# Four weight slots at other byte offsets, and a 2x2 product ahead of 18 runs of matrix products

## The chip, the cores and the metric

The kernel runs on one core of one Trainium2 chip. The metric is the device time of one execution in microseconds (us), the median of several runs. Engines are named as in the profile: PE (TensorE, matrix products), PEld (its weight loads), DVE (VectorE), ACT (ScalarE), POOL (GpSimd) and SP (SyncE, which issues most transfers).

## The reference

Three stages follow each other: a block-causal attention, a feed-forward with a SoLU and a layer norm, and a second feed-forward with a Mish.

```python
scores = np.where(mask, q @ k.T / 8, -1e9)       # 4 x 8 heads, 576 positions, blocks of 64
x = softmax(scores) @ v                          # -> 2304 tokens x 512
h = x @ w_in                                     # 512 -> 1024
solu = h * softmax(h)
ln = (solu - mean(solu)) / sqrt(var(solu) + 1e-6) * g_ln
x = ln @ w_out                                   # 1024 -> 512
h = x @ w2_in                                    # 512 -> 2048
out = (h * tanh(softplus(h))) @ w2_out           # 2048 -> 512
```

All inputs are float32 (some of the weights float64). The kernel keeps the precision by splitting an operand into a high and a low part and adding three products (high by high, high by low, low by high).

## The kernel before, in words

Every operation of the program is first put into a list with an engine, a cost and a priority; a planner (`Plan.order`) then simulates the engines and writes one fixed order for each. The priorities are a table of numbers. Nothing in that table or in the planner's costs is touched here.

The first feed-forward takes 128 tokens at a time. Its first product stands at L864 (output 128 x 512), the transposition of its result at L911, and its second product at L927. `moe1_x2` does the second product for 256 tokens, a group; there are nine groups g. For each group the four 128-column blocks c of the output are worked out in pairs that share a PSUM bank. A block is 8 steps kk of three products, and the planner receives it as two pieces of 12 (k0 = 0 and k0 = 4). So a bank takes 48 products and a group 96, each with a 128 x 128 stationary operand (`woh` or `wol`) and 256 columns of `lth` or `ltl` that stream. In the first two groups the planner mixes the pieces with the attention (scores L694, its products L799 and L806, transpositions L669 and L778); in the seven later groups the 96 products stand in one piece behind L864.

The second feed-forward has its weights in four slots of SBUF. Slot j holds four tiles of 7168 bytes in each partition: `w2ihj`, `w2ohj`, `w2ilj`, `w2olj` (i: first product, o: second, h and l: high and low part). `slot` lays them down, slots 0 and 1 in the pool of `open_right`, slots 2 and 3 in the pool of `open_left`. L1124 is the first product: `w2ih` or `w2il` is stationary, 384 columns of the token blocks (six in the tile `wk`, the seventh in `x7`) stream. L1248 and L1216 are the second product, in the first and in the second half of the stage: there the split activations `ch` and `cl` (or a part of `wk`) are stationary and `w2oh` or `w2ol` streams, 512 columns at L1248, 256 at L1216. In the last part of L1216 spare parts of `w2ih` and `w2il` hold the activations. L1248 comes in pieces of 18 products of one slot (24 such pieces, 6 with each slot); L1216 comes in steps of 3 or 6, and steps of several slots follow each other.

The array's tile, as the instructions give it, is 128 x 128 at L864, L911, L927, L1124, L1216 and L1248 and in all transpositions; 64 x 128 at L694; 128 x 64 at L799; 64 x 64 at L806. The products at L799 and L806 are plain float32, and each is two weight loads and two products in the trace; those of the feed-forwards are float32r and are one.

Of the kernel before, what the change touches and what calls it, by code (L numbers as in the profile page):

```python
# [10 lines left out]
F32 = mybir.dt.float32  # L11
# [67 lines left out]
class Plan:  # L79
# [11 lines left out]
    def add(self, eng, cost, fn, r=(), w=(), prio=0.0, acq=None, rel=None, lat=None, lock=False, mode=0):  # L91
        o = Op()
        o.eng, o.cost, o.fn, o.prio, o.acq, o.rel = eng, cost, fn, prio, acq, rel
        o.lat = self.LAT[eng] if lat is None else lat
        o.lock = lock or eng == POOL
        o.mode = mode
        o.seq = len(self.ops)
        d = set()
        for k in r:
            if k in self.writer:  # L100
                d.update(self.writer[k])
            self.readers.setdefault(k, []).append(o.seq)
        for k in w:
            rd = [x for x in self.readers.get(k, ()) if x != o.seq]
            d.update(rd)
            d.update(self.writer.get(k, ()))
            self.writer[k] = [o.seq]
            self.readers[k] = []
        d.discard(o.seq)
        o.deps = d  # L110

        for k, s in zip(w, acq or ()):
            self.slot[k] = s
        o.on = list({id(self.slot[k]): self.slot[k] for k in (*r, *w) if k in self.slot}.values())
        self.ops.append(o)
        return o
# [144 lines left out]
def c_dma(kb):  # L261
    return max(0.53, kb / 260.0)
# [10 lines left out]
def c_act(n, sbuf=False, acc=False, ptr=False):  # L273
    return 0.05 + n / 1170.0 + 0.04 * sbuf + 0.18 * acc + 0.09 * ptr
# [11 lines left out]
def kernel(  # L286
# [12 lines left out]
    nc = tc.nc  # L299
# [4 lines left out]
    P = 128  # L304
# [15 lines left out]
    def pri(tag, i):  # L320
        base, step = PRIO[tag]
        return base + step * i
# [22 lines left out]
    def ps(s):  # L345
        return banks[s.at // 2][:, s.at % 2, :]
# [4 lines left out]
    ident = const.tile([P, P], F32, name="ident")  # L351
# [165 lines left out]
    def split_weight(src, sk, wd, slot, dh, dl, dk, tag, idx, g=None, gk=None, need=None):  # L517
        pt = dict(prio=pri(tag, idx))
        kw = dict(rel=[slot], **pt) if slot else dict(lock=True, **pt)
        if g is None:  # L520
            add(ACT, c_act(wd, not slot), lambda: act_hi(dh(), src()), r=[sk] + ([need] if need else []),
                w=[dk + ("h",)], **pt)
            if tag == "wi":
                add(POOL, c_tt(wd), lambda: pool_lo(dl(), src(), dh()), r=[sk, dk + ("h",)], w=[dk + ("l",)], **kw)
            else:
                add(DVE, c_dve(wd), lambda: dve_lo(dl(), src(), dh()), r=[sk, dk + ("h",)], w=[dk + ("l",)], **kw)
        else:
            add(ACT, c_act(wd, not slot, ptr=True), lambda: nc.scalar.activation(
                out=dh(), in_=src(), func=AF.Copy, scale=g()), r=[sk, gk], w=[dk + ("h",)], **pt)
            add(DVE, c_dve(wd), lambda: nc.vector.scalar_tensor_tensor(  # L530
                out=dl(), in0=src(), scalar=g(), in1=dh().bitcast(F32), op0=ALU.mult, op1=ALU.subtract),
                r=[sk, gk, dk + ("h",)], w=[dk + ("l",)], **kw)

    def hl(*k):
        return [k + ("h",), k + ("l",)]
# [385 lines left out]
    def moe1_x2(g, lth, ltl):  # L921

        def mm(s, c, k0, k1):
            cs = slice(c * P, (c + 1) * P)
            for kk in range(k0, k1):
                for i, (w, x) in enumerate(((woh, lth), (woh, ltl), (wol, lth))):
                    nc.tensor.matmul(  # L927
                        out=ps(s)[:, (c % 2) * 256:(c % 2) * 256 + 256], lhsT=w[:, kk, cs], rhs=x.t[:, kk, :],
                        start=(kk == 0 and i == 0), stop=(kk == KF - 1 and i == 2))

        for c2 in range(KD // 2):
            s = Slot()
            xo = xo_r.next()
            xk = ("x2", g, c2)
            for cc in range(2):
                for k0 in range(0, KF, 4):
                    first = cc == 0 and k0 == 0
                    add(PE, 12 * 0.1175, lambda s=s, c=2 * c2 + cc, k0=k0: mm(s, c, k0, k0 + 4),
                        r=[x.key(o) for x in (lth, ltl) for o in range(2)]
                        + [y for kk in range(k0, k0 + 4) for y in hl("wo", kk)],  # L940
                        w=[xk] + ([xo.key()] if first else []), acq=[s] if first else None, prio=pri("m_2", 2 * g + 1))
            add(ACT, c_act(512), lambda s=s, xo=xo: nc.scalar.activation(
                out=xo.t, in_=ps(s).rearrange("p (a c) -> p a c", a=2), func=AF.Copy),
                r=[xk], w=[xo.key()], rel=[s], prio=pri("m_o", 2 * g + 1))
            st = add(SP, c_dma(410), lambda c2=c2, xo=xo: nc.sync.dma_start(
                out=x2_d[:, 2 * c2:2 * c2 + 2, g * 256:(g + 1) * 256], in_=xo.t),
                r=[xo.key()], w=[("x2d", g, c2)], prio=pri("store", 0))
            stores.add(st.seq)
# [25 lines left out]
    acc_d = dram.tile([P, NTILE, DM], F32, name="acc_d")  # L974
    RIGHT, MID, LEFT, HALF = "right", "mid", "left", "half"

    def slot(p, j):
        for x in "hl":
            sl_i[j, x] = p.tile([P, 2, 7, P], F32R, name=f"w2i{x}{j}")
            sl_o[j, x] = p.tile([P, 7, 2 * P], F32R, name=f"w2o{x}{j}")  # L980

    def open_right():
        at_cm.__exit__(None, None, None)
        cm = tc.tile_pool(name="m2a", bufs=1, side="right")
        p = cm.__enter__()
        opened["r"] = cm
        for j in range(2):
            slot(p, j)
        xf_r.make(p)
        x7 = p.tile([P, 2 * GT], F32R, name="x7")  # L990
        for i, r in enumerate((blk_h, blk_l)):
            r.tiles = [wk[:, GT * (2 * n + i):GT * (2 * n + i + 1)] for n in range(6)] + [x7[:, GT * i:GT * (i + 1)]]
        g_r[0].make(p, 1)
        p.tile([P, 48], F32, name="edge_f")
        cl_r.make(p, 1)
        p.tile([P, 32], F32, name="edge_g")

    def open_mid():
        ch_r.tiles = [wk[:, 12 * GT + 48:12 * GT + 48 + 7 * P].rearrange("p (a k) -> p a k", a=7)]
# [5 lines left out]
    def open_left():  # L1005
        m1_cm.__exit__(None, None, None)
        cm = tc.tile_pool(name="m2b", bufs=1, side="left")
        p = cm.__enter__()
        opened["l"] = cm
        for j in range(2, NSLOT):  # L1010
            slot(p, j)
        g_r[1].make(p, 4)
        p.tile([P, 48], F32, name="edge_h")
        ch_r.make(p)
        cl_r.make(p)
        ob_r.make(p, 1)
        ob_r.tiles += [t.rearrange("p a b -> p (a b)") for t in xo_r.tiles]
# [384 lines left out]
    for b in range(B):  # L1402
# [5 lines left out]
        while nt < NTILE and (nt + 1) * P <= (b + 1) * S:  # L1408
# [5 lines left out]
            nt += 1  # L1414
    early = len(plan.ops)
    o = add(HOST, 0.0, open_right, w=[RIGHT], prio=-1000)
    o.deps.update(heads)
    o = add(HOST, 0.0, open_mid, w=[MID], prio=-1000)
    o.deps.update(last_use)
    o.deps.add(o.seq - 1)  # L1420
    o = add(HOST, 0.0, open_left, w=[LEFT], prio=-1000)
    o.deps.update(x for x in range(early) if x not in stores)
    o.deps.add(o.seq - 1)
# [78 lines left out]
```

## Time and profile before

| | us |
|---|---|
| median of 3 runs | 777.19 (775.67 to 777.21) |
| profiled execution | 778.42 |
| its span (first to last instruction) | 776.6 |
| PE busy | 758.3 (98%) |
| DVE busy | 574.9 (74%) |
| ACT busy | 446.8 (58%) |
| POOL busy | 250.0 (32%) |

The time around the span is 1.8 us. A busy PE is not a PE at its peak: the products are pipelined, and a row's duration (280 ns for a product of 256 columns) is longer than the step from one start to the next (0.12 us). The step is the quantity to read here, either from the starts in the timeline or from a piece of the chain divided by its count.

### The profile page before, as it was taken

To read this page: it belongs to the slowest core of one execution; us is meant where nothing else is said; L and a number is where in the kernel's file an instruction comes from. 1 tells how busy PE (TensorE), PEld (TensorE's weight loads), DVE (VectorE), ACT (ScalarE), POOL (GpSimd) and SP (SyncE) were. 2 spreads that over 40 slices of the span, in tenths; PEclk is the share of its full clock that TensorE was granted. 3 is DMA by queue.
4 is the path that set the end of the run, shared out by engine and by line. 5 is a ranking of instruction groups with operands and counts; after the bars stand their busy time and mean duration, and the time that the engine had idled before them with its cause. 6 is when DMAs were issued, how large, how long until landed. Compare 5 with 4: busy or idle time off the path is not lost.

```text
span 776.6 us, 14789 instructions
## 1 busy us (share of the span) xinstructions
PE 758.3 (98%) x5496; PEld 688.9 (89%) x5496; DVE 574.9 (74%) x1217; ACT 446.8 (58%) x938; POOL 250.0 (32%) x299
## 2 busy tenths in 40 slices
PE   7898999999999999999999999999999999999997
PEld 6777778788888899999998988988988999999997
DVE  5999898999999896334425897797433679559995
ACT  5898888686666565323428554564444764354560
POOL 1587786784765233232130362222000000000000
PEclk8899999999999999999999999999999999999999
DMA  8664543335335351000376667766696682272303
GB/s 194 165 143 113 136 109 102 115 84 160 105 135 161 95 170 48 28 15 14 122 236 218 225 200 248 279 238 237 228 307 226 200 304 67 84 290 77 95 1 109
DMA packets 108839, 118.13 MB, mean 152 GB/s; under 512 B 66016, under 2 KB 77792, under 8 KB 108768
## 3 DMA queue, kind: packets, MB, share of 16 engines
q1 hardware_dynamic: 107504, 116.88, 48.0%
q8 instruction: 43, 0.70, 0.4%
q10 hardware_dynamic: 1264, 0.31, 0.2%
q14 instruction: 28, 0.23, 0.1%
HBM read 76.27 MB, written 40.89 MB: 151 GB/s over the span
## 4 chain that ended last, share of the span: by engine, by line
PE 86%; DVE 9%; ACT 2%; issue 1%; DMA 1%; SPq 0%; DVEq 0%; ACTq 0%
PE ps L1124 23%; PE ps L864 13%; PE ps L1248 13%; PE ps L927 12%; PE ps L1216 11%; PE ps L694 4%; PE ps L778 3%; PE ps L799 3%; DVE nmx L748 2%; PE ps L911 2%; ACT pt L706 2%; PE ps L806 1%; DVE kl L335 1%; PE ps L669 1%; DVE wem L454 1%
## 5 line engine op out<-in xcount | busy, mean ns | idle before, releaser
L1124 PE MATMUL ps<-wk,w2ih 128*128 128x384 f32 x576 | 147.8, 337 | 1.7 <-ACT xt L1132 1.1
L1124 PEld LDWEIGHTS ps<-wk,w2ih 128*128 128x128 f32 x576 | 102.8, 188 | 4.1 <-ACT xt L1132 1.3
L864 PE MATMUL ps<-wk 128*128 128x512 f32 x432 | 104.6, 396 | 0.0
L762 POOL TENSOR_SCALAR pt<-pt,sm 128x192 f32<-128x192 f32 (+4 forms) x160 | 90.5, 588 | 36.1 <-DVE sm L700 15.1
L511 POOL TENSOR_TENSOR wem<-wem 128x512 f32<-128x512 f32 x40 | 60.7, 1519 | 116.5 <-DVE wem L508 103.0
L706 ACT ACTIVATE pt<-ps,nmx 128x576 f32<-128x576 f32 (+4 forms) x160 | 82.4, 537 | 25.9 <-DVE nmx L748 16.0
L1124 PE MATMUL ps<-wk,w2il 128*128 128x384 f32 x288 | 96.9, 336 | 0.0
L864 PEld LDWEIGHTS ps<-wk 128*128 128x128 f32 x432 | 79.4, 188 | 17.0 <-issue 1.1
L927 PE MATMUL ps<-lth,woh 128*128 128x256 f32 x288 | 81.6, 283 | 0.0
L927 PE MATMUL ps<-lth,wol 128*128 128x256 f32 x288 | 80.9, 281 | 0.0
L927 PE MATMUL ps<-ltl,woh 128*128 128x256 f32 x288 | 80.8, 281 | 0.0
L1248 PE MATMUL ps<-w2oh,cl 128*128 128x512 f32 x144 | 56.8, 395 | 0.0
L927 PEld LDWEIGHTS ps<-lth,wol 128*128 128x128 f32 x288 | 55.0, 191 | 0.0
L927 PEld LDWEIGHTS ps<-lth,woh 128*128 128x128 f32 x288 | 54.2, 188 | 0.9 <-issue 0.5
L1216 PE MATMUL ps<-w2oh,cl 128*128 128x256 f32 x196 | 54.9, 280 | 0.0
L778 PE MATMUL ps<-ident,pt 128*128 128x128 f32 x400 | 50.2, 277 | 4.5 <-DVE kl L335 3.0
L927 PEld LDWEIGHTS ps<-ltl,woh 128*128 128x128 f32 x288 | 54.1, 188 | 0.3
L1124 PEld LDWEIGHTS ps<-wk,w2il 128*128 128x128 f32 x288 | 54.1, 188 | 0.0
L778 PEld LDWEIGHTS ps<-ident,pt 128*128 128x128 f32 x400 | 44.9, 143 | 8.0 <-DVE kl L335 2.8
L748 DVE TENSOR_REDUCE nmx<-ps 128x2 f32<-128x896 f32 (+1 forms) x64 | 41.0, 684 | 0.8
L335 DVE TENSOR_TENSOR ltl<-ps,lth 128x1024 fp32r<-128x1024 f32 x18 | 21.3, 1217 | 26.5 <-ACT lth L329 26.5
L799 PE MATMUL ps<-ptw,vraw 128*64 128x256 f32 (+1 forms) x384 | 39.8, 359 | 0.0
(172 smaller groups left out, 1934.1 us busy)
## 6 DMA issues: line engine op xcount, KB each, us to landing
blk_d<-wk SPq DMA_DIRECT2D x36, 384.0 KB, 4.0
wk<-blk_d SPq DMA_DIRECT2D x36, 384.0 KB, 5.5
wraw<-in_moe_w_in_dram SPq DMA_DIRECT2D x24, 512.0 KB, 4.4
park_d<-wem SPq DMA_DIRECT2D x20, 448.0 KB, 2.8
wraw<-in_moe_w_out_dram SPq DMA_DIRECT2D x16, 512.0 KB, 3.9
wem<-park_d SPq DMA_DIRECT2D x18, 448.0 KB, 4.5
qraw<-in_q_dram SPq DMA_DIRECT2D x30, 160.0 KB, 3.3
x_d<-xo SPq DMA_DIRECT2D x18, 256.0 KB, 2.2
```

The costliest lines, as they stand in the source:

```text
L511: add(POOL, c_tt(wd), lambda: nc.gpsimd.tensor_tensor(out=mf(), in0=mf(), in1=ex().bitcast(F32), op=ALU.mult), r=[ek], w=[mk], **pt)
L694: nc.tensor.matmul(out=dst, lhsT=a.t[hs, t * P:(t + 1) * P], rhs=m.t[hs, o + c0:o + c1], start=(i == 0), stop=(i == 2))
L706: add(ACT, c_act(EXT[t], acc=True), lambda: nc.scalar.activation(out=pp.t[:, x * EXT[t]:(x + 1) * EXT[t]] if t < 4 else pp.t[:, x * EXT[t] ...
L748: add(DVE, 2 * c_dve(512), lambda s=s, ts=ts: [nc.vector.tensor_reduce(out=nmx.t[:, :, t], in_=ps2(s)[:, :, o:o + EXT[t]], axis=AX.X, op=A ...
L762: nc.gpsimd.tensor_scalar(pp, pp, sm.t[:, x, t:t + 1], 1.0, op0=ALU.mult, op1=ALU.mult)
L778: nc.tensor.transpose(ps2(s)[:, a, o:o + P], pts[t].t[:, c * P:(c + 1) * P], ident)
L799: nc.tensor.matmul(out=ps(os_[r])[x * D:(x + 1) * D, o:o + n_], lhsT=vr.t[:, j, x, :], rhs=packs[pi].t[:, a, c0:c0 + n_], start=(i in (0, ...
L864: nc.tensor.matmul(out=ps2(hp)[:, hf, :], lhsT=x.t[:, kk, :], rhs=w[:, kk, hf * 512:(hf + 1) * 512], start=bool(first), stop=bool(last))
L927: nc.tensor.matmul(out=ps(s)[:, (c % 2) * 256:(c % 2) * 256 + 256], lhsT=w[:, kk, cs], rhs=x.t[:, kk, :], start=(kk == 0 and i == 0), stop ...
L1124: nc.tensor.matmul(out=ps(s)[:, 0:HT], lhsT=sl_i[j, w][:, c, a, :], rhs=x.t[:, mv], start=(start and c == 0 and i == 0), stop=(c == 1 and ...
L1216: nc.tensor.matmul(out=ps(acc[bi])[:, h * 256:(h + 1) * 256], lhsT=x.t[:, a], rhs=sl_o[j, w][:, b], start=(first and h == 0 and y == 0), s ...
L1248: nc.tensor.matmul(out=ps(acc[t]), lhsT=x.t[:, 2 * t + f], rhs=plain(j, w, f), start=(first and f == 0 and y == 0), stop=(last and f == 1 ...
```

## The change

Two edits. The first puts a product of two columns by two rows, of plain float32 with start and stop flags, ahead of the first piece (k0 = 0) of blocks 0 and 2 of every group: 18 products. It reads the identity matrix and writes four numbers of the bank that the run behind it overwrites. Its array tile is 128 x 32 in the built program.

The second lays an unused piece ahead of each slot, one behind slots 1 and 3, and makes one existing unused piece 32 bytes smaller.

```diff
         def mm(s, c, k0, k1):
             cs = slice(c * P, (c + 1) * P)
+            if k0 == 0 and c % 2 == 0:
+                nc.tensor.matmul(out=ps(s)[0:2, 0:2], lhsT=ident[:, 0:2], rhs=ident[:, 0:2], start=True, stop=True)
...
+    LEAD = (16, 16, 48, 16)
+    TRAIL = (96, 64)
+
     def slot(p, j):
+        if LEAD[j]:
+            p.tile([P, LEAD[j]], F32, name=f"lead{j}")
...
         for j in range(2):
             slot(p, j)
+        p.tile([P, TRAIL[0]], F32, name="edge_k")
...
-        p.tile([P, 32], F32, name="edge_g")
+        p.tile([P, 24], F32, name="edge_g")
...
         for j in range(2, NSLOT):
             slot(p, j)
+        p.tile([P, TRAIL[1]], F32, name="edge_l")
```

The pool of slots 0 and 1 is laid down from the upper end of SBUF, so it grows downwards. The byte addresses in a partition as built:

| tile | before | remainder by 64 / by 256 | after | remainder by 64 / by 256 |
|---|---|---|---|---|
| slot 0 (`w2ih0`) | 146592 | 32 / 160 | 146176 | 0 / 0 |
| slot 1 (`w2ih1`) | 175264 | 32 / 160 | 174912 | 0 / 64 |
| slot 2 (`w2ih2`) | 72384 | 0 / 192 | 72576 | 0 / 128 |
| slot 3 (`w2ih3`) | 101056 | 0 / 192 | 101312 | 0 / 192 |
| `x7` | 216224 | 32 / 160 | 216256 | 0 / 192 |
| `cl0` | 225632 | 32 / 96 | 225664 | 0 / 128 |
| `ch1` | 136064 | 0 / 128 | 136576 | 0 / 128 |
| `cl1` | 139648 | 0 / 128 | 140160 | 0 / 128 |
| `wk` (not moved) | 5824 | 0 / 192 | 5824 | 0 / 192 |

A slot's four tiles have the same remainders, since 7168 is a multiple of 256; the second product at L1248 reads `w2oh` and `w2ol` from 192 bytes behind their start.

On PE, the third group's run of L927 stands directly behind L864 before:

```order
L864 MATMUL ps_63<-wk 128x512 [waits DVE_49]
L864 MATMUL ps_63<-wk 128x512 x23
L927 MATMUL ps_64<-lth_144,woh 128x256 [waits DVE_49,Activation_49]
L927 MATMUL ps_64<-ltl_145,woh 128x256
L927 MATMUL ps_64<-lth_144,wol 128x256
L927 MATMUL ps_64<-lth_144,woh 128x256
```

and after, with the same products now at L929, on PE at the same place:

```order
L864 MATMUL ps_63<-wk 128x512 [waits DVE_49]
L864 MATMUL ps_63<-wk 128x512 x23
L926 MATMUL ps_64<-ident 2x2 [waits DVE_49,Activation_49]
L929 MATMUL ps_64<-lth_144,woh 128x256 [waits Activation_49]
L929 MATMUL ps_64<-ltl_145,woh 128x256
L929 MATMUL ps_64<-lth_144,wol 128x256
L929 MATMUL ps_64<-lth_144,woh 128x256
```

The wait for the bank is now the 2x2 product's, the wait for the split operand stays with the run. In the middle of the same group, on PE, where the second pair of blocks begins, the order before is:

```order
L927 MATMUL ps_64<-lth_144,wol 128x256
L927 MATMUL ps_64<-lth_144,woh 128x256 [waits DVE_49]
L927 MATMUL ps_64<-ltl_145,woh 128x256
L927 MATMUL ps_64<-lth_144,wol 128x256
L927 MATMUL ps_64<-lth_144,woh 128x256
```

and after, on PE at the same place:

```order
L929 MATMUL ps_64<-lth_144,wol 128x256
L926 MATMUL ps_64<-ident 2x2 [waits DVE_49]
L929 MATMUL ps_64<-lth_144,woh 128x256
L929 MATMUL ps_64<-ltl_145,woh 128x256
L929 MATMUL ps_64<-lth_144,wol 128x256
```

One run of 96 becomes two of 48, each with a 2x2 product ahead. Of the 18 new products, two stand in the first group, behind L694 and behind L806; the other sixteen stand behind products with an array tile of 128 x 128 (L864, L1124, or the run's own). On DVE, ACT, POOL and SP no instruction is added, removed or moved.

## Rows read from the trace of the kernel before

**Rows 1.** The page: engines, and the chain that ended last by engine and line

```profile
PE 758.3 (98%) x5496; PEld 688.9 (89%) x5496; DVE 574.9 (74%) x1217; ACT 446.8 (58%) x938; POOL 250.0 (32%) x299
...
PE 86%; DVE 9%; ACT 2%; issue 1%; DMA 1%; SPq 0%; DVEq 0%; ACTq 0%
```

**Rows 2.** The chain in order of time (start us, us, what), around one group

```profile
278.92 10.92 PE ps L864 x48
289.85 11.31 PE ps L927 x96
301.15 1.75 PE ps L911 x16
```

**Rows 3.** The chain between 176 and 199 us, in the first group

```profile
187.91 1.38 DVE nmx L722 x2
189.30 0.60 DVE wem L508
189.90 1.72 DVE wem L1054 x3
```

**Rows 4.** L927, 265.8 to 277.1 us: duration ns min/median/max, first and last start

```profile
L927 PEld LDWEIGHTS ps<-lth,wol x32: 192/192/192, 265.8 to 276.8; 128*128 128x128 f32 x32
L927 PE MATMUL ps<-lth,wol x32: 281/281/283, 265.9 to 276.9; 128*128 128x256 f32 x32
```

**Rows 5.** L927 likewise, 182.1 to 185.0 us

```profile
L927 PEld LDWEIGHTS ps<-lth,wol x8: 187/188/188, 182.4 to 184.8; 128*128 128x128 f32 x8
L927 PE MATMUL ps<-lth,wol x8: 276/276/301, 182.5 to 184.9; 128*128 128x256 f32 x8
```

**Rows 6.** L927 likewise, from 186.5 us, from 231.3 and from 237.8

```profile
L927 PE MATMUL ps<-lth,wol x8: 276/276/283, 186.8 to 189.2; 128*128 128x256 f32 x8
...
L927 PE MATMUL ps<-lth,wol x4: 280/281/281, 231.6 to 232.6; 128*128 128x256 f32 x4
...
L927 PE MATMUL ps<-lth,wol x4: 276/277/281, 238.1 to 239.2; 128*128 128x256 f32 x4
```

**Rows 7.** Timeline of PE (start us, us, what): from L927 to L799

```profile
178.79 0.28 PE L927 MATMUL ps<-ltl,woh 128*128 128x256 f32 x1
178.90 0.28 PE L927 MATMUL ps<-lth,wol 128*128 128x256 f32 x1
179.11 0.44 PE L799 MATMUL ps<-ptw,vraw 128*64 128x256 f32 x2
```

**Rows 8.** Timeline of PE: all of L806, then L927, first starts and last

```profile
181.42 0.80 PE L806 MATMUL ps<-ptw,vraw 64*64 64x64 f32 x20
182.15 0.39 PE L927 MATMUL ps<-lth,woh 128*128 128x256 f32 x1
182.37 0.28 PE L927 MATMUL ps<-ltl,woh 128*128 128x256 f32 x1
...
182.84 0.28 PE L927 MATMUL ps<-lth,wol 128*128 128x256 f32 x1
...
184.88 0.30 PE L927 MATMUL ps<-lth,wol 128*128 128x256 f32 x1
```

**Rows 9.** The chain: pieces of L1248 with slots 1, 2, 3 and 0

```profile
427.54 4.19 PE ps L1248 x18
...
443.28 4.17 PE ps L1248 x18
...
470.25 4.10 PE ps L1248 x18
...
480.67 4.17 PE ps L1248 x18
```

**Rows 10.** The chain: L1124 with slots 0 and 1, 2 and 3, and 0, 1, 2, 1

```profile
535.89 7.36 PE ps L1124 x42
...
559.04 8.35 PE ps L1124 x48
...
598.56 9.51 PE ps L1124 x54
```

**Rows 11.** The chain: L1216 with slots 0 and 1, then 1 and 2

```profile
639.61 2.46 PE ps L1216 x21
...
643.12 2.51 PE ps L1216 x21
```

## The prediction

> **What bounds the kernel now.** I read the page's engine line and the chain's shares first: PE is busy for 98% of the span and holds 86% of the chain, DVE 9% [rows 1]. Then the chain in order of time. From the third group on, one group is 48 products of L864, 96 of L927 and 16 transpositions, back to back, with nothing of another engine between them [rows 2]. There, time added to PE is added to the end. In the first group it is otherwise: between 176 and 199 us the chain runs through DVE [rows 3], so that what PE does more there lies beside other work. In the second feed-forward the chain is again PE alone. What counts is therefore the step from one product's start to the next.
>
> Taken that way, L927 has two paces. A run of 96 takes 11.31 us [rows 2], a step of 117.8 ns; seven groups have such a run. The run between 182 and 185 us goes from 182.84 to 184.88 in 18 steps [rows 8], 113.3 ns each. The rows tell the paces apart: in the slow one each load of `wol` takes 192 ns and a product 281 [rows 4], in the quick one 188 and 276 [rows 5]. All tiles and addresses are the same in both. The pace is thus a matter of how the run starts, and it keeps itself up.
>
> **The 2x2 products: what one costs.** The trace has no array tile of 128 x 32, but it has changes of tile. Four pieces:
> - leaving a run of 128 x 128: from the last start of L927 to L799's first, 178.90 to 179.11, 0.21 us [rows 7].
> - from the first pass of the float32 product to its second. L806 starts 181.42 and its 20 passes, in 10 pairs, end after 0.80 [rows 8]; with a last pass of 0.22 that leaves 0.58 for nine steps, 0.06 each. A stationary operand of 2 columns instead of 64 should need less; I take 0.03, between 0.01 and 0.11.
> - from the last pass to the run. L806's last pair starts at 182.00, the run at 182.15: 0.15, of which about 0.05 is the streaming of 64 columns [rows 8]. I take 0.10, at most 0.15.
> - the run's first step, in which nothing was loaded ahead: 182.15 to 182.37, 0.22 [rows 8].
>
> That is 0.56 us, in place of two ordinary steps of 0.118: 0.325 each, between 0.30 and 0.45 (high end 0.21 + 0.11 + 0.15 + 0.22 - 0.24). Sixteen stand on the chain, 5.2 us (4.8 to 7.2). The two of the first group stand behind L694 and L806, where the tile changes anyway, and beside DVE's chain: nothing. Were that cover gone they would cost some 0.15 each.
>
> The Trainium skill, TensorEngine Tiling (Array Packing), Key Properties, says that a change of the tiling mode drains the engine, which would hold for 128 x 32 as it does for the 128 x 64 of [rows 7]; without a drain the sum would be the third rival's below. No row of the trace has the 32.
>
> **What the run behind one gains.** After a change of tile the run between 182 and 185 us needs four steps from 182.37 to 182.84, 0.47 us [rows 8], which is the slow pace, and is quick from there on. So 43 of 48 products gain 4.4 ns, 0.19 us. Fourteen such runs in the last seven groups give 2.66; the second group, 48 and 12, about 0.22; the first is largely quick already and off the chain. 2.9 us, if every run turns quick. That is not certain: of five runs of the first two groups that stand behind L694 or L806, four turn quick (three of them are the runs from 182, 186.5 and 237.8 us [rows 5, 6]), but the one at 231 us, behind L694, keeps products of 281 ns [rows 6]. Ends: 0 and 2.9. I take 2.9, because the sixteen heads are alike, and the two runs behind L806, the nearest thing to a small float32 product, both turn.
>
> **The moved slots.** At L1248 a piece of 18 takes 4.10 us with slot 3, but 4.19, 4.17 and 4.17 with slots 1, 2 and 0 [rows 9]. Slots 3 and 1 stream past the same `ch1` and `cl1`; only the slots' place differs. With slot 3 every operand starts at a multiple of 64 bytes; with 0 and 1 the slot is off by 32, with slot 2 `cl0` is. After the change all are multiples of 64. If that is what counts, 6 pieces gain 0.09 and 12 gain 0.07: 1.4 us. At L1124 the pieces with slots 2 and 3 take 174.0 ns a step (8.35 by 48), those with 0, 1, 2, 1 176.1 (9.51 by 54), with 0 and 1 175.2 (7.36 by 42) [rows 10]. 504 products use slots 0 and 1: between 0.6 and 1.1 us; I take 0.6. At L1216 pieces of 21 take 2.46 or 2.51 us with no order by slots [rows 11]; nothing, within -0.4 and +1.4 (36 pieces, 0.04 each). Together a gain of 2.0, with ends of 2.9 gained and, should the new spread by 64 put all pieces where the slowest are, a loss: at L1248 6 x (0.02 + 0.02 + 0.09) = 0.8, at L1124 504 x 2.1 ns = 1.1, so 1.9.
>
> The Trainium skill, TensorE: Matmul & The Clock Gate, Part 2, says that PE reads SBUF through two independent ports, one for the streamed operand and one for weight loads. By that rule loads and streams cannot meet and addresses would be worth nothing. The trace does not agree: 4.10 and 4.19 us for the same `ch1` and `cl1` [rows 9]. It stays a rival, since other things differ between these pieces too.
>
> **The sum.** 5.2 - 2.9 - 2.0 = +0.3 us on the profiled execution's 778.42 (span 776.6 and 1.8 around it): 778.7. The median of the runs shown is 777.19, 1.2 below that execution; on it the forecast is 777.5 us, no change that could be told. A measurement of this kernel tells a change from none from about 0.2% on, 1.55 us.
>
> **Rivals.**
> 1. The runs stay slow behind the 2x2 product (slower). Place: the sixteen heads of L927. For it: the run at 231 us [rows 6], and that the pace hangs on a few nanoseconds at the start. Against it: the two behind L806, from 182 and 237.8 us [rows 5, 6]. 5.2 - 2.0 = +3.2, so 780.4. It decides from seven heads of sixteen that do not turn, since each takes 0.19 off the gain.
> 2. Addresses are worth nothing: 5.2 - 2.9 = +2.3, 779.5. For it: L1216 shows no order. Against it: [rows 9].
> 3. The 2x2 product does not drain the array and costs about one step of L806, 0.05: 16 x 0.05 - 2.9 - 2.0 = -4.1, 773.1. Against it: each change of tile in the trace costs its 0.1 on either side [rows 7, 8].
> 4. The new spread of the slots hurts: 5.2 - 2.9 + 1.9 = +4.2, 781.4. No product of 384 or 512 columns in the trace has operands 64 or 128 apart by 256, so nothing bears it out; nothing excludes it.
>
> **How the numbers follow.** Forecast 0.44; rival 1 0.20, 2 0.12, 3 0.12, 4 0.08, the rest 0.04. The forecast's own range is 776.2 to 779.8: its low end takes 0.4 less for the products, 0.5 more at L1124 and 0.4 at L1216, its high end 2.0 more for the products and 0.3 less from the runs. Slower: rivals 1 and 4, most of 2, and 0.07 of the forecast's high end, 0.44. Faster: rival 3, 0.05 of the forecast and 0.02 of the rest, 0.19. Within: 0.37. The range goes from 775.0 to 781.2, which leaves out rival 3 and half of rival 4.
>
> **What would show it.** Chain: runs of 96 at L927 that become two of 48, each about 0.2 us shorter than half of 11.31, with 0.33 between. Rows of L927: products of 276 and loads of `wol` of 188 ns say quick; 281 and 192 say rival 1. Timeline around a 2x2 product: 0.21, 0.03, 0.10 and 0.22 from start to start; far less would be rival 3. L1248: all pieces of 18 near 4.10; 4.17 to 4.19 as before say rival 2, longer ones rival 4. The prediction is wrong if DVE or ACT shows up between the groups on the chain, or if L1216, which I set at nothing, moves by more than 1 us.

## The result and the profile after

The changed kernel takes 781.02 us (median of five runs, 779.64 to 782.34); the kernel before takes 777.19 (median of five, 775.67 to 778.27). The ratio is 1.0054, with an interval of 1.0043 to 1.0066: slower by 3.8 us, where 0.3 was forecast. The profiled execution took 781.02 us, its span is 779.2.

The page after, with the engines' line and the chain's shares:

```profile
PE 761.9 (98%) x5532; PEld 688.8 (88%) x5532; DVE 574.0 (74%) x1217; ACT 446.6 (57%) x938; POOL 250.4 (32%) x299
...
PE 86%; DVE 10%; issue 1%; ACT 1%; DMA 1%; SPq 0%; DVEq 0%; ACTq 0%
```

It is the picture of [rows 1] with 36 more products (two for each 2x2). No other engine came onto the chain, so the time has to be looked for in PE's own steps. The chain around one group (start us, us, what) answers to [rows 2]:

```profile
278.81 10.93 PE ps L864 x48
289.74 0.12 PE ps L926 x2
289.86 5.66 PE ps L929 x48
295.52 0.12 PE ps L926 x2
295.64 5.86 PE ps L929 x48
```

The run of 96 took 11.31 us [rows 2]. Its two halves with their heads now take 0.12 + 5.66 + 0.12 + 5.86 = 11.76, so a group is 0.45 longer. The halves are not alike: the second takes 0.20 more than the first. The products show why. First the first half of the group that begins at 265.3 us, then its second half; the columns are those of [rows 4]:

```profile
L929 PE MATMUL ps<-ltl,woh x16: 276/276/278, 265.6 to 270.7; 128*128 128x256 f32 x16
...
L929 PE MATMUL ps<-ltl,woh x16: 281/281/281, 271.4 to 276.7; 128*128 128x256 f32 x16
```

276 is the quick pace [rows 5], 281 the slow one [rows 4]. The first half turns quick and the second is slow, in all the groups behind L864; not one is quick throughout. The granted clock is 1.00 (2.4 GHz) from 100 us on in both traces, so it is not the clock that parts the two paces. The timeline of PE (start us, us, what) around the second head of that group:

```profile
270.81 0.28 PE L929 MATMUL ps<-lth,wol 128*128 128x256 f32 x1
271.01 0.19 PE L926 MATMUL ps<-ident 128*2 128x2 f32 x2
271.13 0.38 PE L929 MATMUL ps<-lth,woh 128*128 128x256 f32 x1
271.36 0.28 PE L929 MATMUL ps<-ltl,woh 128*128 128x256 f32 x1
```

From 270.81 to 271.01 is 0.20, from there to the run 0.12 (0.03 between the two passes and 0.09 behind), and the run's first step 0.23: 0.55 us in place of two ordinary steps, 0.24. A head costs 0.31.

The last of the seven groups stands behind L1133 and goes the other way, slow first and then quick (the chain):

```profile
396.58 3.18 PE ps L1133 x18
399.76 0.12 PE ps L926 x2
399.88 5.85 PE ps L929 x48
405.73 0.12 PE ps L926 x2
405.85 5.67 PE ps L929 x48
```

The moved slots. Pieces of L1257 (L1248 before) with slots 1, 2, 3 and 0, which answer to [rows 9]:

```profile
430.14 4.17 PE ps L1257 x18
...
445.90 4.20 PE ps L1257 x18
...
472.82 4.11 PE ps L1257 x18
...
483.25 4.13 PE ps L1257 x18
```

Slots 1 and 0 gain 0.02 and 0.04, slot 2 loses 0.03, slot 3 0.01. All four start at a multiple of 64 bytes now, and they still differ. L1133 (L1124 before), the same three pieces as in [rows 10], and two of L1225 (L1216 before) as in [rows 11]:

```profile
538.41 7.36 PE ps L1133 x42
...
561.52 8.38 PE ps L1133 x48
...
601.07 9.48 PE ps L1133 x54
...
642.17 2.46 PE ps L1225 x21
...
645.68 2.41 PE ps L1225 x21
```

These pieces move by 0.03 or less in L1133 and by 0.10 at most in L1225. Summed over all steps from start to start in the two traces, L1133 is 0.16 us longer than L1124 was, L1225 0.19 longer, L1257 0.21 shorter: +0.14 in all.

The account of the two profiled executions: the third group begins at 265.31 us in the chain after and at 265.87 before, so 0.56 earlier; seven groups cost 0.45 each, 3.1; the slots 0.14. That makes 2.7, and the spans differ by 779.2 - 776.6 = 2.6. The earlier start need not be the change's work: in the first 50 us the granted clock was 0.90 on average in the trace before and 0.93 in the trace after. The other 1.2 between 2.6 and the medians' 3.8 is what the profiled execution of before lay above its median.

### The profile page after: what moved, and what is told of

Its sections match the earlier page's. It is cut to its first block, busy times and chain, and to the rows that moved or that the text cites. A ratio compares the mean times of both kernels' runs of the same rounds, so it can differ in the third digit from the quotient of the medians.

```text
span 779.2 us, 14857 instructions
## 1 busy us (share of the span) xinstructions
PE 761.9 (98%) x5532; PEld 688.8 (88%) x5532; DVE 574.0 (74%) x1217; ACT 446.6 (57%) x938; POOL 250.4 (32%) x299
## 4 chain that ended last, share of the span: by engine, by line
PE 86%; DVE 10%; issue 1%; ACT 1%; DMA 1%; SPq 0%; DVEq 0%; ACTq 0%
PE ps L1133 23%; PE ps L864 13%; PE ps L1257 13%; PE ps L929 12%; PE ps L1225 11%; PE ps L799 3%; PE ps L694 3%; PE ps L778 3%; DVE nmx L748 2%; PE ps L911 2%; PE ps L806 1%; DVE kl L335 1%; DVE nmx L722 1%; PE ps L669 1%; DVE wem L454 1%
## 5 line engine op out<-in xcount | busy, mean ns | idle before, releaser
L1133 PE MATMUL ps<-wk,w2ih 128*128 128x384 f32 x576 | 147.9, 338 | 1.7 <-ACT xt L1141 1.1
L1133 PEld LDWEIGHTS ps<-wk,w2ih 128*128 128x128 f32 x576 | 102.9, 188 | 4.0 <-ACT g L1141 1.3
L864 PE MATMUL ps<-wk 128*128 128x512 f32 x432 | 104.7, 396 | 0.0
L1133 PE MATMUL ps<-wk,w2il 128*128 128x384 f32 x288 | 97.0, 337 | 0.0
L864 PEld LDWEIGHTS ps<-wk 128*128 128x128 f32 x432 | 79.4, 188 | 17.1 <-issue 1.1
L929 PE MATMUL ps<-lth,woh 128*128 128x256 f32 x288 | 82.7, 287 | 0.0
L929 PE MATMUL ps<-lth,wol 128*128 128x256 f32 x288 | 80.2, 278 | 0.0
L929 PE MATMUL ps<-ltl,woh 128*128 128x256 f32 x288 | 80.1, 278 | 0.0
L1257 PE MATMUL ps<-w2oh,cl 128*128 128x512 f32 x144 | 56.6, 393 | 0.0
L929 PEld LDWEIGHTS ps<-lth,woh 128*128 128x128 f32 x288 | 54.4, 189 | 1.0 <-issue 0.3
L1225 PE MATMUL ps<-w2oh,cl 128*128 128x256 f32 x196 | 55.0, 281 | 0.0
L929 PEld LDWEIGHTS ps<-lth,wol 128*128 128x128 f32 x288 | 54.1, 188 | 0.0
L929 PEld LDWEIGHTS ps<-ltl,woh 128*128 128x128 f32 x288 | 54.1, 188 | 0.0
L1133 PEld LDWEIGHTS ps<-wk,w2il 128*128 128x128 f32 x288 | 54.0, 188 | 0.0
L799 PE MATMUL ps<-ptw,vraw 128*64 128x256 f32 (+1 forms) x384 | 39.8, 358 | 0.0
```

Of the source, the lines that this page charges most:

```text
L799: nc.tensor.matmul(out=ps(os_[r])[x * D:(x + 1) * D, o:o + n_], lhsT=vr.t[:, j, x, :], rhs=packs[pi].t[:, a, c0:c0 + n_], start=(i in (0, ...
L864: nc.tensor.matmul(out=ps2(hp)[:, hf, :], lhsT=x.t[:, kk, :], rhs=w[:, kk, hf * 512:(hf + 1) * 512], start=bool(first), stop=bool(last))
L929: nc.tensor.matmul(out=ps(s)[:, (c % 2) * 256:(c % 2) * 256 + 256], lhsT=w[:, kk, cs], rhs=x.t[:, kk, :], start=(kk == 0 and i == 0), stop ...
L1133: nc.tensor.matmul(out=ps(s)[:, 0:HT], lhsT=sl_i[j, w][:, c, a, :], rhs=x.t[:, mv], start=(start and c == 0 and i == 0), stop=(c == 1 and ...
L1225: nc.tensor.matmul(out=ps(acc[bi])[:, h * 256:(h + 1) * 256], lhsT=x.t[:, a], rhs=sl_o[j, w][:, b], start=(first and h == 0 and y == 0), s ...
L1257: nc.tensor.matmul(out=ps(acc[t]), lhsT=x.t[:, 2 * t + f], rhs=plain(j, w, f), start=(first and f == 0 and y == 0), stop=(last and f == 1 ...
```

## The experiments

**The two edits apart.** The kernel before with the 2x2 products alone:

```diff
+            if k0 == 0 and c % 2 == 0:
+                nc.tensor.matmul(out=ps(s)[0:2, 0:2], lhsT=ident[:, 0:2], rhs=ident[:, 0:2], start=True, stop=True)
             for kk in range(k0, k1):
```

> The 18 products of 2x2 alone, slots where they were before. Theory: the extra time is the sixteen products on the chain, 0.31 us each (5.0), less 0.19 for each run of 48 that turns quick, and only those behind L864 turn (8: 1.5), so +3.5 us on before; L1124, L1216 and L1248 step as before. Rival, the moved slots cost the time: at most +1.5 us here.

Measured 779.72 us against 776.50, ratio 1.0038 (1.0026 to 1.0051), that is 3.0 us of 776.5 (the medians are 3.2 apart), where 3.5 were expected. The halves behind L864 are 5.66 and 5.86 as after. And the moved slots alone, without the products:

> The moved slots alone, no product of 2x2. Theory: what slots 0 and 2 gain at one of L1124 and L1248, slots 1 and 2 lose at the other, so within 0.5 us of before; L927 at 11.31 us a run of 96. Rival, the moved slots cost the time: +1.5 to +2.5 us. Rival, the 2x2 products hid a gain of the slots: -2.0 us.

Measured 776.67 against 776.50, ratio 1.0001 (0.9991 to 1.0010). So the loss lies with the 2x2 products, and the slots bring nothing. The two edits are not quite separate: the last group's run, which is slow in the kernel before (11.32 us in its chain), is quick in this one without any head:

```profile
396.83 10.90 PE ps L927 x96
```

**Which head turns a run.** Only the first head of a group stays:

```diff
+            if k0 == 0 and c == 0:
+                nc.tensor.matmul(out=ps(s)[0:2, 0:2], lhsT=ident[:, 0:2], rhs=ident[:, 0:2], start=True, stop=True)
```

> Before with the 2x2 product only ahead of block 0: nine, of which eight are on the chain. Theory, a run keeps the pace it has until something interrupts it: 8 x 0.31 = 2.5 us for the products, 91 of 96 steps quicker by 4.4 ns in seven or eight runs, 2.8 to 3.2, so -0.5 us on before, within -1 and +0.2; a run of 96 at 10.9 us and its head included at 11.2. Rival, the second bank falls back by itself to 117.8 ns: only 43 of 96 gain, 1.5, so +1.0 us.

Measured 776.67 against 776.50, ratio 0.9996 (0.9986 to 1.0007). The chain of one group:

```profile
288.60 0.12 PE ps L926 x2
288.72 11.10 PE ps L929 x96
```

All 96 products are quick now: the change of bank in the middle does not undo the pace. 11.22 us with the head against 11.31 is 0.09 a group, which the medians can't tell from nothing. Then only the second head:

```diff
+            if k0 == 0 and c == 2:
+                nc.tensor.matmul(out=ps(s)[0:2, 0:2], lhsT=ident[:, 0:2], rhs=ident[:, 0:2], start=True, stop=True)
```

> Before with the 2x2 product only ahead of block 2, in the middle of each run of 96, where the run in front of it is a slow one. Theory P (what stands in front decides): behind a slow run it turns like behind L864, so of 48 products 43 at 113.3 ns, 8 x (0.31 - 0.19) = +1.0 us on before. Theory B (the block decides: block 2 starts badly whatever is in front): all of the 48 stay at 117.8, 8 x 0.31 = +2.5 us.

Measured 778.05 against 777.18, ratio 1.0014 (1.0003 to 1.0025). The chain:

```profile
288.29 5.65 PE ps L929 x48
293.95 0.12 PE ps L926 x2
294.07 5.66 PE ps L929 x48
```

The two halves are each as long as the other, but the first has no head and the second has one, whose slow first step is in its 5.66. After the change a second half behind a head took 5.86. The products of the two halves of this group (columns as in [rows 4]):

```profile
L929 PE MATMUL ps<-ltl,woh x16: 281/281/281, 288.2 to 293.6; 128*128 128x256 f32 x16
...
L929 PE MATMUL ps<-ltl,woh x16: 276/276/283, 294.2 to 299.3; 128*128 128x256 f32 x16
```

Slow, then quick. After the change the same second head stood behind products of 276 ns and left products of 281; here it stands behind 281 and leaves 276. What stands in front decides, not the place.

**Addresses: one remainder for all.** The kernel before with one unused piece 32 bytes smaller, which brings slots 0 and 1 and `x7` to the remainder 192 by 256 that slots 2, 3 and `wk` have, and `cl0` to the 128 of `ch1` and `cl1`:

```diff
-        p.tile([P, 32], F32, name="edge_g")
+        p.tile([P, 24], F32, name="edge_g")
```

> Before with the unused piece edge_g 32 bytes smaller and nothing else: then all four slots, x7 and the blocks in wk have remainder 192 by 256, and w2oh and w2ol behind their 192 bytes, ch and cl 128, as slot 3 alone has before. Theory, what counts is the distance of the stationary and the streamed address by 256: all pieces of 18 of L1248 near 4.10 us (-1.4), L1124 near 174.0 ns (-0.6), so -2.0 us. Rival, slot 3 is quick for another reason (its place, its time): 4.17 to 4.19 stay with slots 0 to 2, 0 us.

Measured 773.65 against 776.50, ratio 0.9963 (0.9950 to 0.9976), -2.9 us. The chain: L1248 with slots 1, 2, 3 and 0, and L1124 with 0, 1, 2, 1:

```profile
424.71 4.09 PE ps L1248 x18
...
440.32 4.09 PE ps L1248 x18
...
467.10 4.09 PE ps L1248 x18
...
477.43 4.09 PE ps L1248 x18
...
594.06 9.39 PE ps L1124 x54
```

All four pieces of L1248 are as quick as slot 3's was [rows 9], and the piece of L1124 comes down from 9.51 to 9.39 [rows 10]. Over all steps L1248 gives 1.45 us, L1124 0.93, L1216 costs 0.24, and the last group's run of L927 is quick (10.89), 0.4: 2.5 of the 2.9. A multiple of 64 alone can't be what slots 0 and 1 lacked, for in the changed kernel all slots have it and are not equally quick. What sorts both kernels is the distance, by 256 bytes, of the stationary from the streamed operand. In the changed kernel that distance is 64, 128, 192 and 0 at L1133 for slots 0 to 3, and 192, 128, 64 and 0 at L1257; the mean steps there, worked out from the starts in the trace, are about 175, 176, 174 and 174 ns, and 229, 231, 233 and 228. With 0 and 192 they are low, with 64 and 128 high. Of the three new distances one is nearly as good as 0 and two are worse. At 384 and 512 columns this is not the only sorting that fits: slots that are read at a remainder of 128 or 192 are low and those read at 0 or 64 high, in both products, whatever stands against them. That the partner's address counts too shows in slot 2, which this edit leaves where it was and which gains with `cl0`; more no run tells at these lengths. At 256 columns the next runs do.

**The same on L927**, where the distance of `woh` from `lth` is 64 in the kernel before. An unused piece ahead of `lth` of 32, 48 or no elements in place of 16 makes it 0, 192 or 128:

```diff
-    m1.tile([P, 16], F32, name="edge_e")
+    m1.tile([P, 32], F32, name="edge_e")
```

> Before with lth and ltl 64 bytes higher (edge_e 32 elements), no 2x2 product, slots as before: distance of woh's and lth's address by 256 then 0 instead of 64. Theory (256 columns: the distance sets the step, as L1216 shows in the kernel after: 119.5 ns at 0, 116.3 at 64, 118.7 at 128, 117.4 at 192): L927 at 119 to 120 ns, +1.0 to +1.8 us. Rival (distance 0 is the good one for every width, as at L1248): 113.3 ns without any product ahead, -3.3 us.

> The same with lth and ltl 128 bytes higher (edge_e 48 elements): distance 192. Theory: 117.4 ns, -0.3 us, within 0.7 of before. Rival (0 and 192 are the good ones, as at L1124 and L1248): 113.3 ns, -3.3 us.

> The same with lth and ltl 64 bytes lower (edge_e left out): distance 128. Theory: 118.7 ns, +0.8 us. Rival, the distance has nothing to do with it: 117.8 ns as before, 0 us.

Measured 778.47, 777.12 and 778.88 us against 777.18: 1.0018 (1.0008 to 1.0027) for 0, 0.9998 (0.9989 to 1.0008) for 192, 1.0019 (1.0009 to 1.0030) for 128. For 128, 0.8 us was expected, half of what came. The run of 96 in the chain, 11.31 us at 64, for distance 0, for 192 and for 128 (where the line is L926):

```profile
288.64 11.51 PE ps L927 x96
```

```profile
289.22 11.31 PE ps L927 x96
```

```profile
286.75 11.52 PE ps L926 x96
```

Only addresses differ, and seven groups at 0.2 are the 1.3 to 1.7 us. For 256 streamed columns 0 is bad, where it is good for 384 and 512: the order of the four distances is another one there. And it is the distance that counts at 256 columns: L1216 in the kernel with one remainder has `ch` and `cl` at 128 and `w2oh` and `w2ol` at 192, the run at distance 192 here has, by the layout, `woh` at 192 and `lth` at 0; both step at 117.8 ns, with rows of 279 to 280 ns that are neither of the two of [rows 4] and [rows 5]. No head was tried at 0, 192 or 128.

**Two remainders.** So the first product's slots stay 0 from `wk`, and the second product's at L1216, with 256 columns, are put 64 from `ch` and `cl`:

```diff
+        p.tile([P, 32], F32, name=f"gap_i{j}")
+        for x in "hl":
             sl_o[j, x] = p.tile([P, 7, 2 * P], F32R, name=f"w2o{x}{j}")
+        p.tile([P, 32], F32, name=f"gap_o{j}")
...
-        return sl_o[j, x].rearrange("p a k -> p (a k)")[:, 48 + f * DM:48 + (f + 1) * DM]
+        return sl_o[j, x].rearrange("p a k -> p (a k)")[:, 16 + f * DM:16 + (f + 1) * DM]
```

> Slots laid out so that w2ih and w2il keep remainder 192, and w2oh and w2ol begin at 64 (L1248 still reads at 128, from 64 bytes behind the start): at L1216 the distance is then 64 in place of 0 or 192 (128 in place of 0 where spare parts of w2ih and w2il are stationary). Theory (256 columns: 116.4 ns at 64, 117.7 at 192, 118.7 at 128, 119.9 at 0): 588 steps quicker by 1.3 ns, 168 by 1.2, so 1.0 us less than with one remainder, -3.8 us on before. Rival, 64 was good only by the way its pieces began: -2.85.

Measured 773.59 against 777.33, ratio 0.9953 (0.9941 to 0.9966). That interval overlaps the one of one remainder, so the medians don't tell the two apart; by the steps L1219 (L1216 before) gives 1.25 us more than with one remainder and L1127 (L1124) gives 0.44 of it back. L1219 in the chain, against the 2.46 and 2.51 of [rows 11]:

```profile
605.36 2.47 PE ps L1219 x21
...
640.40 2.39 PE ps L1219 x21
...
643.85 2.39 PE ps L1219 x21
```

These products have the distance of L927 before, 64, and they show the two paces of L927, though no head stands ahead of any of them. The rows of an early piece and of a later one (columns as in [rows 4]):

```profile
L1219 PE MATMUL ps<-w2oh,cl x6: 281/281/282, 624.3 to 626.0; 128*128 128x256 f32 x6
...
L1219 PE MATMUL ps<-w2oh,cl x6: 276/276/278, 644.9 to 647.7; 128*128 128x256 f32 x6
```

With one remainder, distance 192, all the products of that line but those of the last stretch (spare parts as stationary operand) keep 117.8 ns. So the quick pace of 113.3 ns was seen at distance 64 alone, in two lines.

**The one remainder, or the two, with the first 2x2 head.** Both should have added e3's small gain (the edit is e3's, on top of either kernel).

> The two edits that did something good, together: all slots at remainder 192 (edge_g 24) and one 2x2 product ahead of block 0 of each group. Theory: they touch different stages and add, -2.85 measured for the first and -0.3 (-0.5 by the steps) for the second, -3.2 us on before. Rival: the head is worth nothing beside it, -2.8.

> All three: w2i at 192, w2o at 64, and one 2x2 product ahead of block 0 of each group. Theory: -3.8 and -0.4 add to -4.2 us on before. Rival, as for its parts: -3.2.

Measured 775.02 and 773.76 against 777.33: 0.9969 (0.9957 to 0.9980) and 0.9952 (0.9940 to 0.9965). With the one remainder the medians are 2.3 us apart instead of the expected 3.2, with the two the head adds nothing to be seen, instead of 0.4. Both intervals still hold what was expected, so it is the chain of the last group that shows a loss (one remainder, with the head):

```profile
396.79 0.12 PE ps L926 x2
396.92 11.52 PE ps L929 x96
```

Without the head this run is quick in both kernels (10.89 us in their chains). With it, it is slow, with the two remainders as well (11.52). That costs 0.75 (11.52 + 0.12 - 10.89), more than the 0.5 that the other six groups give at 0.09 each.

**A head without a change of tile.** The same two columns, but with the whole identity as stationary operand, so that the array's tile stays 128 x 128:

```diff
+            if k0 == 0 and c == 0:
+                nc.tensor.matmul(out=ps(s)[:, 0:2], lhsT=ident, rhs=ident[:, 0:2], start=True, stop=True)
```

> As the run with one head a group, slots as before, but the head is a float32 product with the whole identity as its stationary operand and 2 columns: its array tile is 128 x 128, so that no tile changes. Theory D (the drain at the change of tile resets the pace): the run stays at 117.8 ns, and two loads of 128 columns cost 0.2 us each time, +1.6 us on before. Rival F (a float32 product of two passes turns the pace, drained or not): 8 x (0.2 - 0.4) = -1.6 us.

Measured 775.32 against 777.33, ratio 0.9976 (0.9967 to 0.9985). The timeline of PE at one head:

```profile
287.35 0.28 PE L926 MATMUL ps<-ident 128*128 128x2 f32 x2
287.49 0.36 PE L929 MATMUL ps<-lth,woh 128*128 128x256 f32 x1
287.69 0.28 PE L929 MATMUL ps<-ltl,woh 128*128 128x256 f32 x1
```

From 287.35 to 287.69 is 0.34 in place of one step of 0.12: this head costs 0.22, with no wait ahead of it. The run behind it is quick all the same:

```profile
287.51 0.12 PE ps L926 x2
287.63 11.00 PE ps L929 x96
```

11.12 us against 11.31, and all seven runs are so. The pace turns without any change of tile. With two such heads a group (`c % 2 == 0`):

> The heads where the change has them, ahead of blocks 0 and 2, but each of 128 x 128 by 2 columns, so that no array tile changes; slots as before. Theory A (a head turns the pace over, whatever it was): the second 48 of each group are slow again, 16 x 0.22 - 8 x 0.19 = +2.0 us on before. Theory B (only the wait for the empty array drops a quick run): the whole run stays quick, 16 x 0.22 - 8 x 0.40 = +0.3 us.

Measured 779.02 against 777.02, ratio 1.0028 (1.0017 to 1.0039). The chain of a group:

```profile
288.80 5.56 PE ps L929 x48
294.36 0.12 PE ps L926 x2
294.47 5.76 PE ps L929 x48
```

Quick and then slow again, as with the 2x2. A second head of either kind throws away what the first one won.

**The best of both.** The two remainders with one full-tile head a group:

> w2i at remainder 192, w2o at 64, and one head a group of 128 x 128 by 2 columns. Theory: -3.65 for the remainders and -1.9 for the head add, -5.5 us on before. Rival, the remainders upset the run behind L1124 as they did with the 2x2 product: -5.1. Rival, the parts do not add, as for the run with both and a 2x2 product: -3.7.

Measured 772.78 against 777.02, ratio 0.9944 (0.9931 to 0.9957): the quickest of all, 4.2 us below the kernel before, where 5.5 less was expected. All seven runs are quick. The head's part of it, a further 0.7 by the two ratios, is within the intervals.

## Why the prediction was wrong, step by step

- **What bounds the kernel** was right. PE's steps set the time, no DVE or ACT appeared between the groups, and the two heads of the first group cost nothing that can be seen.
- **What a 2x2 product costs** was right: 0.31 each against 0.325, in the pieces 0.20, 0.03, 0.09 and 0.23 against 0.21, 0.03, 0.10 and 0.22. Sixteen are 5.0 us. Rival 3, no drain, is out: the step ahead of the 2x2 is 0.20. The head that keeps the tile costs 0.22 and not 0.31; since it also loads 128 columns in place of 2, the price of the change of tile by itself stays open. One reading in that sum was wrong: 0.06 is the step from one pair of passes of L806 to the next, and the two passes of a pair start 0.01 apart in that trace. That the 0.03 taken for it was met is luck.
- **"2.9 us, if every run turns quick"** is the step that failed. Half of the runs turn. A head did not set the pace, it turned it over: behind 48 products at the slow pace the next 48 are quick, behind quick ones they are slow. That was seen behind L864 in every group, with either half alone (the first and the second head apart), with both kinds of heads, and in the last group, where with the slots moved the run without a head is quick and with one slow. One of each pair turns: 8 x 0.19 = 1.5 in place of 2.9, a miss of 1.4 us. The reason given, "because the sixteen heads are alike", is the mistake. The heads were alike, the runs in front of them were not: half of them stood behind products that by the same forecast had just become quick. The working asked what a head does to products at 117.8 ns a step and never what it does to those at 113.3. Rival 1 named the right place, with a wrong rule (nothing turns). Its price of 3.2 lies near the 3.8 measured by luck, since it counts a gain of 2.0 from the slots that did not come. The stated range, up to 781.2, holds the 781.0 for no better reason: the forecast's own part ended at 779.8, and what lies above stood for rivals 1 and 4, neither of which happened.
- **"If that is what counts"**, a multiple of 64, 2.0 us from the moved slots: the second failure, and in size the larger: moving them cost 0.14, a miss of 2.1 us. The slots' order in [rows 9] was an effect of addresses, as argued, but what sorts it is the distance of the two operands by 256 (at 384 and 512 columns the slots' own remainder by 256 would do as well). The one smaller gap alone, which makes that distance 0, gave 2.9, and the same shift plus the new leads, of which two slots have a bad distance, gave nothing. The table of remainders by 256 stood ahead of the prediction; the remainder by 64 was chosen because it sufficed to sort four slots. Rival 4 was right that the new spread can hurt and too dear by far (1.9 of loss where 0.14 was lost), since 192 is nearly as good as 0.
- **The Trainium skill**, TensorE: Matmul & The Clock Gate, Part 2, has loads and streams on independent ports, and the prediction drew from it that addresses would be worth nothing. The runs go against that for this case: with nothing but addresses changed, the same 96 products took 11.31 or 11.51 us.
- **The sum** with the measured terms is 5.0 - 1.5 + 0.14 = +3.6, and +3.8 was measured.

What stays open: what in PE keeps a run at 113.3 or 117.8 ns a step, why the quick one was seen at distance 64 alone, and why a small float32 product turns the one into the other. Two cases do not fit the rule of turning over, both in the last group, behind the first product of the second feed-forward, and both with the full-tile head: with the two remainders the run is quick without a head and stays quick with one (11.01 us), and with two heads in the kernel before it is slow first (5.76) and then quick. Neither was run again to tell why. Nor was it tried to find out why 0 bytes of distance are good for 384 and 512 columns and bad for 256.

## What to carry to other kernels

Where the same instructions run at two paces, ask of an inserted instruction what it does to a run that is quick already, and try it once and twice: an effect that depends on the state in front can cancel itself. A change of addresses that sorts the existing pieces by one remainder should be checked against the next larger one and against the distance of the two operands that meet, and be measured with one address moved at a time. And two edits whose terms nearly cancel should be weighed as two: the sum hid that both gains hung on an "if".

## What the runs showed of the hardware

- The step of a float32r product with a 128 x 128 stationary operand goes with the distance of the stationary from the streamed address by 256 bytes. At 256 columns it is 113.3 or 117.8 ns at 64 (L927; 2.39 and 2.47 us for 21 products of L1219), 117.8 at 192 (L927, L1216), 119.9 at 0 and at 128 (L927; at 128 in the last group 118.8). At 384 columns it is about 174 at 0 and 192, 175 to 176 at 64 and 128 (L1133), at 512 columns 228 and 229 at 0 and 192, 231 and 233 at 128 and 64 (L1257); there the slots' own remainder is not excluded as the cause.
- A float32 product of two columns turns the pace of the float32r run behind it from 117.8 to 113.3 ns or back, and the run keeps it for 96 products and over a change of bank (11.10 us with one head). It does so with a change of tile (0.31 us) and without one (0.22 us). Two runs of the last group did not follow.
